# The opening stage of attention and two MLPs: all five engines in written order, weight preparation taken apart into single steps

## The chip, the cores and the metric

The kernel runs on one core of one Trainium2 chip. The metric is the device time of one execution in microseconds. Three runs of the kernel before took 616.21, 618.01 and 620.59 us; the median, 618.01 us, is the time that the change is measured against.

## What is computed

A decayed linear attention over 2 batches, 8 heads, 768 positions and 64 channels, then two MLPs on its 1536 tokens of 512 channels: one gated by a sigmoid (1536 wide), one with an ELU (2048 wide). All in float32.

```python
for b in range(nb):                       # blocks of the sequence
    intra = (qb @ kb.T * Dmask) @ vb
    inter = (qb * lam_pow) @ kv_state
    out[:, :, sl] = intra + inter
    kv_state = lam_block * kv_state + (kb * rev_pow).T @ vb
x = attention output as (tokens, 512)
x = (sigmoid(x @ w_gate) * (x @ w_val)) @ w_out
h = x @ w_in
y = where(h > 0, h, exp(min(h, 0)) - 1) @ w_out2
```

## The kernel before

The weights arrive as 64-bit floats; each load brings 1 MB (`load_w`, line 61) into the one buffer `w64`. `fetch` turns it into float32 in the one buffer `w32` with three instructions: ScalarE L71, VectorE L72 and L73. A later load of weights waits in SP's queue until L73 of the one before has read `w64`. Each float32 product is made of three matmuls of float32r halves, high and low, and the input products of the MLPs use a seven-product scheme (M1 to M7, line 181; one such product on 256 tokens is one step of six matmuls, and `ORDER` is the order in which the steps run). `prep_pair` therefore forms sums of weight blocks on GpSimd (t25 at L81, three parts of t3 at L83 to L85), rounds them to high halves on ScalarE (L91) and forms the low halves on VectorE or GpSimd (L92). The first two blocks of weights, of gate (wG) and value (wV), are needed as soon as two chunks of attention are done.

The opening stage handles the sequence in six chunks c of 128 positions. For each chunk and batch b (written here as two digits after the name: x10 is x of chunk 1, batch 0):

- TensorE: u (the chunk's part of the state, L300), st (scores, L287), x (output, L317, and from chunk 1 on L322 for the part from the state).
- ScalarE: kd (keys times decay, 8 instructions, L276), the copies of x to `xa` (L327, L329), the high halves of x (`x11h`, `x22h`, L142), of sums (`x143h`) and of xt (`xPh`, both L153).
- VectorE: pr (scores times mask, L293), sn (state, L307, L310), the low halves of x (L143), sums (L147), xt (L149).
- GpSimd: ql (queries times decay, L280, two buffers, released by x), and the low halves `x143l` and `xPl` (L154).

The stage has three groups of 14 steps of the MLP (gate, then value, each M2 M5 M1 M4 M3 M7 M6), on tokens of chunks 0 and 1, 2 and 3, 4 and 5. They become available after chunks 1, 3 and 5, and `fill(k)` puts the next k of them into TensorE's order between the attention's matmuls; what is left runs after chunk 5. While nothing of that kind is available (chunks 0 and 1), `warm_up(3)` puts three matmuls on zeros there, 24 in all, besides the 24 ahead of the loop.

In this stage only TensorE and SP (which issues every DMA) run in the order in which the program stands; a planner orders the other three engines by its own estimate of times, with high priority for attention. After chunk 5 (`start.close()`) it orders all engines.

SP's order before: lam, tin and nat of chunk 0 (tin in two halves), w_gate block 0, tin and nat of chunk 1, of chunk 2, w_val block 0, chunk 3, and so on. tin holds keys and queries, nat keys and values.

Of the kernel before, what the change touches and what calls it, by code (L numbers as in the profile page):

```python
# [30 lines left out]
def tile_decay_attention_two_mlps(  # L31
# [32 lines left out]
    def fetch(src, g, raw=None):  # L64

        raw = load_w(src, g) if raw is None else raw
        w = ws_p.tile([P, 1024], F32, tag="w32", name="w32")
        wi = w.bitcast(U32)  # L70
        nc.scalar.activation(w, raw[:, :, 1].bitcast(F32), AF.Prelu, scale=2.0 ** -112, alpha=2.0 ** 32)  # L71
        nc.vector.tensor_scalar(out=wi, in0=wi, scalar1=3, scalar2=None, op0=ALU.logical_shift_left)  # L72
        nc.vector.scalar_tensor_tensor(out=wi, in0=raw[:, :, 0], scalar=29, in1=wi,  # L73
                                       op0=ALU.logical_shift_right, op1=ALU.bitwise_or)
        return w

    def prep_pair(src, g, eng, eng_l=None, raw=None):
        eng_l = eng_l or eng
        raw = fetch(src, g, raw).rearrange("p (k a f) -> p k a f", k=KC, a=2)
# [6 lines left out]
        r = {}  # L86

        def split(tag, x, shape):
# [6 lines left out]
        h, l = split("25", t25, [P, 2, 2, P])  # L95
        r["M2"] = (h[:, :, 1], l[:, :, 1])
        r["M5"] = (h[:, :, 0], l[:, :, 0])
        h, l = split("3", t3, [P, 3, 2, P])
        r["M1"] = (h[:, 0], l[:, 0])
        r["M6"] = (h[:, 1], l[:, 1])  # L100
        r["M7"] = (h[:, 2], l[:, 2])
        r["M4"] = split("22", raw[:, 2:4, 1], [P, 2, P])
        r["M3"] = split("11", raw[:, 0:2, 0], [P, 2, P])
        return r

# [28 lines left out]
    def build_from_psum(ops, s, x0, x1, xa, t0, n, sums):  # L134


        sl = slice(t0, t0 + n)
        o = ops[s]
        a, b = slice(0, 2), slice(2, 4)
        with tc.high_priority(offset=HP):  # L140
            for key, src in (("11", x0[:, a]), ("22", x1[:, b])):
                nc.scalar.copy(o[key, "h"][:, :, sl], src)  # L142
                nc.vector.tensor_tensor(out=o[key, "l"][:, :, sl], in0=src, in1=o[key, "h"][:, :, sl].bitcast(F32),  # L143
                                        op=ALU.subtract)
            for k, (i0, i1, op) in enumerate(((x1[:, b], xa[:, a], ALU.add), (x0[:, b], xa[:, a], ALU.subtract),
                                              (x1[:, a], xa[:, 4:6], ALU.subtract))):
                nc.vector.tensor_tensor(out=sums[:, k], in0=i0, in1=i1, op=op)  # L147
            t = t_p.tile([P, 512], F32, tag="xt", name="xt", bufs=3).rearrange("p (k n) -> p k n", k=KC)
            nc.vector.tensor_tensor(out=t, in0=x1, in1=xa[:, 0:KC], op=ALU.add)  # L149
        for key, src, view in (("143", sums, (slice(None),) * 3), ("P", t, (slice(None),) * 2)):  # L150
            hi_, lo_ = (o[key, q][view + (sl,)] for q in "hl")
            with tc.high_priority(offset=HP):
                nc.scalar.copy(hi_, src)  # L153
                nc.gpsimd.tensor_tensor(out=lo_, in0=src, in1=hi_.bitcast(F32), op=ALU.subtract)  # L154
# [63 lines left out]
    with ExitStack() as actx:  # L218
# [4 lines left out]
        start.enter_context(tc.manual_schedule(engines={mybir.EngineType.PE, mybir.EngineType.SP}))  # L223
# [29 lines left out]

        one = low[:, 1536:1536 + CH]
# [17 lines left out]
        def front_pre(c):  # L272
# [4 lines left out]
            if c:  # L277
# [61 lines left out]

        idle = t_p.tile([P, 512], F32, tag="xt", name="idle", bufs=3).bitcast(BF16)[:, :512]  # L340
        nc.vector.memset(idle, 0.0)
# [8 lines left out]
        front_pre(0)  # L350
# [4 lines left out]
        wG = prep_pair(w_gate, 0, nc.gpsimd, nc.vector, w64)  # L355
        load(2)
        for c in range(NCH):
            if c == 0:
                wV = prep_pair(w_val, 0, nc.gpsimd, nc.gpsimd)
            more = c + 1 < NCH  # L360
            with tc.high_priority(offset=HP):
                if more:
                    state_mm(c)
                    state_post(c)
                    front_pre(c + 1)
                for b in range(2):
                    out_mm(c, b)
                    if c <= FIRST[0]:
                        warm_up(3)
                    if b == 0:  # L370
                        fill(2)
                    elif more:
                        fill(3)
                    if more:
                        front_mm(c + 1, b)
                        front_post(c + 1, b)
                    if c <= FIRST[0]:
                        warm_up(3)
                if c + 3 < NCH and c < 2:
                    load(c + 3)  # L380
                if c == 3:
                    load(c + 2)
            if c == 1:
                xops += new_xops(1)
# [3 lines left out]
            s, t0 = (0, c * CH) if c < 2 else (1, (c - 2) * CH)  # L388
            build_from_psum(xops, s, xps[c, 0], xps[c, 1], xas[c], t0, CH,
                            a2_p.tile([P, 3, 2, CH], F32, tag="sums", name="sums"))  # L390
# [124 lines left out]
    wG = prep_pair(w_gate, 1, nc.gpsimd)  # L515
# [146 lines left out]
```

## Time and profile before

| | |
|---|---|
| median of three runs | 618.01 us |
| the profiled execution | 620.34 us |
| its span, first to last instruction | 618.6 us |
| TensorE busy | 594.6 us, 96% |
| VectorE, ScalarE, GpSimd busy | 398.4, 298.7, 319.0 us |
| mean granted clock of TensorE | 0.986 of full |
| chunk 5's last x ends | 80.0 us into the span |

Busy times add the durations of instructions on one engine. Matmuls overlap in their records, so a TensorE that counts as busy may still wait. The granted clock is 1.00 at 2.4 GHz and 0.50 at 1.2 GHz; a mean between them is a stretch with both. The chain of work that ended last is followed back from the last instruction, at each step to what released it.

### The profile page before, as it was taken

The page shows a single profiled execution, that of the slowest core. Times are in us where ns is not written, and L with a number is a line of the kernel's source. Part 1 is how long each engine was busy: PE and PEld are TensorE (multiplying, and loading weights), DVE is VectorE, ACT ScalarE, POOL GpSimd, SP SyncE. Part 2 cuts the span into 40 slices and gives each one's busy share as a digit, 9 for nine tenths or more (in the row PEclk, how much of TensorE's full clock was granted, in tenths as well). Part 3 has the DMA queues.
Part 4 walks back from the last instruction along what each step waited for, and adds up shares of the span by engine and source line. Part 5 has one row for each costly group of instructions (what it writes and reads, how often), then busy time and mean ns, then how long its engine had stood idle before and what let it go on. Part 6 is the DMA issues. An engine that isn't in the chain of part 4 may idle for free.

```text
span 618.6 us, 9255 instructions
## 1 busy us (share of the span) xinstructions
PE 594.6 (96%) x3609; PEld 503.6 (81%) x3614; DVE 398.4 (64%) x681; ACT 298.7 (48%) x565; POOL 319.0 (52%) x262
## 2 busy tenths in 40 slices
PE   8899899999999999999997799979999999999997
PEld 4588799888888888888886688858888888888886
DVE  5979455455556465647746886565868676777574
ACT  3783246555415423515315868763728282816330
POOL 1788345968647538438335865663545445421100
PEclk9899899999999999999998999989999999999999
DMA  8935002323111111112300120421111211100005
GB/s 329 413 144 206 1 1 78 129 83 122 69 68 69 69 68 69 69 68 73 133 0 2 43 93 1 136 70 68 69 68 69 69 68 70 68 1 1 0 18 187
DMA packets 8828, 51.98 MB, mean 84 GB/s; under 512 B 1104, under 2 KB 1360, under 8 KB 3024
## 3 DMA queue, kind: packets, MB, share of 16 engines
q1 hardware_dynamic: 8784, 51.39, 22.4%
q8 instruction: 28, 0.46, 0.3%
q14 instruction: 16, 0.13, 0.1%
HBM read 48.24 MB, written 3.15 MB: 83 GB/s over the span
## 4 chain that ended last, share of the span: by engine, by line
PE 83%; DVE 9%; ACT 4%; issue 2%; DMA 1%; SPq 0%; DVEq 0%; ACTq 0%
PE xu L446 33%; PE A L181 19%; PE B L181 19%; PE C L181 6%; DVE w L72 2%; PE st L287 1%; DMA nat<-in_att 1%; PE x L322 1%; ACT kd L276 1%; PE x L317 1%; DVE w L73 1%; DVE acc L457 1%; ACT w L71 1%; DVE wt L190 1%; PE u L300 0%
## 5 line engine op out<-in xcount | busy, mean ns | idle before, releaser
L446 PE MATMUL xu<-gh,woh 128*128 128x512 f32 x310 | 120.8, 393 | 3.5 <-DVE acc L457 2.0
L457 DVE TENSOR_TENSOR acc<-xu,acc 128x512 f32<-128x512 f32 x120 | 81.9, 687 | 61.3 <-PE xu L446 60.6
L446 PE MATMUL xu<-gl,woh 128*128 128x512 f32 x310 | 120.8, 390 | 0.0
L446 PE MATMUL xu<-gh,wol 128*128 128x512 f32 x310 | 120.2, 388 | 0.0
L417 POOL TENSOR_TENSOR gl<-sig,gh 128x1024 fp32r<-128x1024 f32 (+1 forms) x38 | 79.2, 2100 | 41.5 <-ACT gh L416 41.5
L92 POOL TENSOR_TENSOR l<-t,h 128x512 fp32r<-128x512 f32 (+1 forms) x36 | 59.0, 1640 | 33.5 <-ACT h L91 28.5
L446 PEld LDWEIGHTS xu<-gh,woh 128*128 128x128 f32 x310 | 58.2, 189 | 16.7 <-DVE acc L457 4.4
L446 PEld LDWEIGHTS xu<-gh,wol 128*128 128x128 f32 x310 | 58.4, 188 | 12.2
L446 PEld LDWEIGHTS xu<-gl,woh 128*128 128x128 f32 x310 | 58.5, 189 | 10.4
L91 ACT CAST h<-t 128x512 fp32r<-128x512 f32 (+1 forms) x40 | 29.1, 730 | 54.3 <-POOL t L81 32.1
L92 POOL TENSOR_TENSOR l<-w,h 128x256 fp32r<-128x256 f32 x36 | 26.7, 748 | 55.5 <-ACT h L91 54.3
L73 DVE SCALAR_TENSOR_TENSOR w<-w,w 128x1024 uint32<-128x1024 uint32 x34 | 52.0, 1529 | 0.2
L416 ACT CAST gh<-sig 128x512 fp32r<-128x512 f32 (+1 forms) x58 | 43.8, 783 | 12.1 <-DVE sig L202 10.5
L190 DVE TENSOR_TENSOR wt<-B,wt 128x256 f32<-128x256 f32 (+1 forms) x44 | 22.6, 515 | 40.7 <-PE B L181 32.8
L72 DVE TENSOR_SCALAR w<-w 128x1024 uint32<-128x1024 uint32 x34 | 34.7, 1021 | 21.0 <-ACT w L71 20.9
L426 POOL TENSOR_TENSOR wol<-w,woh 128x512 fp32r<-128x512 f32 x26 | 33.1, 1297 | 29.2 <-ACT woh L424 29.1
L81 POOL TENSOR_TENSOR t<-w 128x512 f32<-128x512 f32 x20 | 26.0, 1302 | 38.5 <-DVE w L73 38.5
L71 ACT ACTIVATE w<-w 128x1024 f32<-128x1024 f32 x34 | 38.7, 1139 | 14.6 <-POOL l L92 7.2
L204 ACT ACTIVATE sig<-A 128x256 f32<-128x256 f32 (+1 forms) x34 | 16.0, 471 | 50.9 <-PE A L181 32.8
L91 ACT CAST h<-w 128x256 fp32r<-128x256 f32 x40 | 16.0, 407 | 47.2 <-PE A L181 22.7
L181 PE MATMUL A<-x11h,h 128*128 128x256 f32 (+1 forms) x88 | 29.8, 338 | 9.0 <-DVE sig L202 5.4
L205 ACT ACTIVATE sig<-sig 128x256 f32<-128x256 f32 (+1 forms) x68 | 34.2, 507 | 1.5
(169 smaller groups left out, 1566.0 us busy)
## 6 DMA issues: line engine op xcount, KB each, us to landing
w<-in_w_out SPq DMA_DIRECT2D x14, 1024.0 KB, 4.8
w<-in_w_in SPq DMA_DIRECT2D x8, 1024.0 KB, 4.7
nat<-in_att SPq DMA_DIRECT2D x6, 1024.0 KB, 9.6
w<-in_w_gate SPq DMA_DIRECT2D x6, 1024.0 KB, 4.8
w<-in_w_val SPq DMA_DIRECT2D x6, 1024.0 KB, 4.8
tin<-in_att SPq DMA_DIRECT2D x5, 1024.0 KB, 10.3
out_t<-o SPq DMA_DIRECT2D x11, 256.0 KB, 2.0
tin<-in_att SPq DMA_DIRECT2D x2, 512.0 KB, 4.8
```

What stands on the lines that cost most here:

```text
L71: nc.scalar.activation(w, raw[:, :, 1].bitcast(F32), AF.Prelu, scale=2.0 ** -112, alpha=2.0 ** 32)
L72: nc.vector.tensor_scalar(out=wi, in0=wi, scalar1=3, scalar2=None, op0=ALU.logical_shift_left)
L73: nc.vector.scalar_tensor_tensor(out=wi, in0=raw[:, :, 0], scalar=29, in1=wi, op0=ALU.logical_shift_right, op1=ALU.bitwise_or)
L91: nc.scalar.copy(hi, x)
L92: eng_l.tensor_tensor(out=lo, in0=x, in1=hi.bitcast(F32), op=ALU.subtract)
L181: nc.tensor.matmul(ps, lhsT=a[:, k], rhs=b_[:, k], start=first and k == 0 and j == 0, stop=k == 1 and j == 2, skip_group_check=True,)
L205: nc.scalar.add(dst, dst, -1.0)
L416: nc.scalar.copy(h, x)
L417: ((eng0 if s == 0 else eng) or eng or nc.gpsimd).tensor_tensor(out=l, in0=x, in1=h.bitcast(F32), op=ALU.subtract)
L426: (eng or nc.gpsimd).tensor_tensor(out=lo_[:, k], in0=raw[:, k], in1=hi_[:, k].bitcast(F32), op=ALU.subtract)
L446: nc.tensor.matmul(ps, lhsT=w[:, k, cs], rhs=g_cols(g, q, k, t_)[:, bs], start=k == 0 and j == 0, stop=k == 1 and j == 2)
L457: nc.vector.tensor_tensor(out=v, in0=p, in1=v, op=ALU.add)
```

## The change

In the opening stage every engine now runs in the order in which the program stands. `fetch` and `prep_pair` become generators (`fetch_steps`, `sum_steps`) whose steps the loop asks for one at a time, and `build_from_psum` is taken apart into the methods of `Operands`. The first step of wG (L71) stands after the keys of chunk 1, its L72 and L73 in chunk 1, its sums and halves at the end of chunk 1; wV is fetched in chunk 2 and split in chunk 3 (its load stands in chunk 1); block 1 of w_gate is fetched at the end of chunk 4, where the planner was free to take it earlier. Low halves of wG's and wV's t25 and single blocks are on VectorE, those of t3 on GpSimd. In SP's order chunk 1 now stands ahead of w_gate block 0. A small ScalarE instruction on a zeroed element stands at the very start, and the first load of the ScalarE table with it. The 24 `warm_up` matmuls inside the loop are gone, those ahead of it stay. `fill` puts in 3 steps in chunk 2 (5 before), 5 each in chunks 3 and 4, and 2 in chunk 5, so 15 of the 42 (17 before) stand inside the loop.

```diff
-        start.enter_context(tc.manual_schedule(engines={mybir.EngineType.PE, mybir.EngineType.SP}))
+        start.enter_context(tc.manual_schedule())
...
+        nc.vector.memset(low[:, 1664:1665], 0.0)
+        nc.scalar.mul(low[:, 1665:1666], low[:, 1664:1665], 1.0)
...
-        w64 = load_w(w_gate, 0)
         load(1)
+        w64G = load_w(w_gate, 0)
...
-        wG = prep_pair(w_gate, 0, nc.gpsimd, nc.vector, w64)
         load(2)
+        raw, wG, wV, raw1, parts = {}, {}, {}, {}, {}
+        fG = fetch_steps(w64G, raw)
         for c in range(NCH):
+            more = c + 1 < NCH
+            s, t0 = (0, c * CH) if c < 2 else (1, (c - 2) * CH)
+            if more:
+                state_mm(c)
+                if c != 2:
+                    queries(c + 1)
+            out_mm(c, 0)
+            o = parts[c] = Operands(xops, s, t0, CH, xas[c], a2_p.tile([P, 3, 2, CH], F32, tag="sums", name="sums"))
+            o.hi("11", xps[c, 0][:, 0:2])
+            if c == 1:
+                parts[0].split("143")
+            elif more:
+                state_post(c)
+            if c != 1:
+                o.first(xps[c, 0])
+            if more:
+                keys(c + 1)
             if c == 0:
-                wV = prep_pair(w_val, 0, nc.gpsimd, nc.gpsimd)
...
+                next(fG)
             if c == 1:
+                sG = sum_steps(raw["w"], wG, nc.gpsimd, nc.vector, nc.gpsimd, (0, 2, 1))
+            if c == 2:
+                parts[1].split("143")
+                queries(3)
+                parts[1].split("P")
+            if c > 2:
+                fill(2)
+            if more:
+                front_mm(c + 1, 0)
+                if c == 1:
+                    next(fG)
+                front_post(c + 1, 0)
+            if c == 1:
+                next(fG)
+                next(sG)
+                parts[0].split("P")
+                state_post(c)
+                o.first(xps[c, 0])
+                w64V = load_w(w_val, 0)
+            if c == 2:
+                fV = fetch_steps(w64V, raw)
+                next(fV)
+            out_mm(c, 1)
+            o.hi("22", xps[c, 1][:, 2:4])
+            if c == 3:
+                for _ in sV:
+                    pass
+            if c > 1 and more:
+                fill(3)
+            if more:
+                front_mm(c + 1, 1)
+                front_post(c + 1, 1)
+            o.second(xps[c, 1])
+            if c == 1:
+                for _ in sG:
+                    pass
                 xops += new_xops(1)
...
+            if c == 2:
+                for _ in fV:
+                    pass
+                sV = sum_steps(raw["w"], wV, nc.gpsimd, nc.vector, nc.gpsimd, (0, 2, 1))
+                next(sV)
+            if c > 1:
+                o.split("143")
+                o.split("P")
+            if c in (0, 1, 3):
+                load(3 if c == 0 else 4 if c == 1 else 5)
+            if c == 4:
+                wG1 = fetch(w_gate, 1)
...
-    wG = prep_pair(w_gate, 1, nc.gpsimd)
+    wG = prep_sums(wG1, nc.gpsimd)
```

The new steps that the loop calls (`hi` rounds one block of x on ScalarE, `lo` and the sums run on VectorE, `split` is ScalarE, then GpSimd):

```python
def first(self, x0):      # sums[:, 1], then lo("11")
def second(self, x1):     # sums[:, 0], sums[:, 2], xt, then lo("22")
def split(self, key):     # "143" or "P": high half, low half
```

## Rows read from the trace of the kernel before

**Rows 1.** The page's busy times, shares of the span and counts of each engine.

```profile
PE 594.6 (96%) x3609; PEld 503.6 (81%) x3614; DVE 398.4 (64%) x681; ACT 298.7 (48%) x565; POOL 319.0 (52%) x262
```

**Rows 2.** Windows: start:end, length, busy us (instructions) per engine, clock, DMA share, GB/s.

```profile
11.45:22.00 10.55, 8.23 (x91) 5.43 (x91) 7.61 (x11) 7.84 (x23) 7.45 (x6) 1.00 1.01 422
22.00:26.00 4.00, 3.64 (x42) 2.64 (x45) 3.58 (x8) 2.10 (x4) 0.41 (x2) 0.62 1.01 420
...
38.58:68.50 29.92, 29.01 (x389) 25.76 (x388) 23.05 (x44) 14.33 (x33) 23.69 (x20) 1.00 0.30 114
68.50:74.20 5.70, 3.86 (x27) 3.21 (x25) 2.42 (x7) 1.72 (x3) 3.20 (x3) 0.70 0.00 0
...
80.00:100.00 20.00, 19.73 (x160) 19.29 (x161) 9.97 (x22) 12.00 (x26) 11.23 (x9) 1.00 0.04 9
100.00:200.00 100.00, 100.00 (x527) 86.00 (x526) 52.88 (x87) 47.43 (x77) 69.86 (x57) 1.00 0.26 94
```

**Rows 3.** The same view of the warm-up matmuls alone (L346), from u00 on.

```profile
11.45:79.96 68.51, 6.20 (x21) 1.77 (x24) 0.95 0.50 198
```

**Rows 4.** The chain that ended last, pieces in time: start us, us, what.

```profile
2.16 7.28 DMA nat<-in_att
9.51 1.28 ACT L276
10.80 2.45 ACT kd L276 x8
...
14.36 0.71 DVE w L72
...
17.19 0.68 DVE sn L307
...
18.53 2.24 DVE l L92 x2
...
81.59 0.73 PE A L181 x6
```

**Rows 5.** Timeline of TensorE, landmarks: start us, us, engine line op out<-in.

```profile
26.37 1.04 PE L317 MATMUL x<-pr,nat 128*64 128x128 f32 x16
...
36.59 1.04 PE L317 MATMUL x<-pr,nat 128*64 128x128 f32 x16
...
46.77 1.15 PE L300 MATMUL u<-nat,kd 128*64 128x64 f32 x32
...
55.96 0.38 PE L181 MATMUL A<-x11h,h 128*128 128x256 f32 x1
...
72.17 2.08 PE L287 MATMUL st<-tin 64*128 64x128 f32 x16
...
78.87 1.09 PE L322 MATMUL x<-ql,sn 64*64 64x128 f32 x16
```

**Rows 6.** Timeline of VectorE and GpSimd around 44 us, [idle before].

```profile
43.51 1.32 POOL L280 TENSOR_TENSOR ql<-tin,low 128x512 f32<-128x512 f32 x1
...
43.67 4.73 DVE L72 TENSOR_SCALAR w<-w 128x1024 uint32<-128x1024 uint32 x1 [0.98 <-ACT w L71]
...
46.55 1.29 POOL L280 TENSOR_TENSOR ql<-tin,low 128x512 f32<-128x512 f32 x1
```

**Rows 7.** Groups, 11.45 to 80 us: shapes xcount | busy us, mean ns | idle before.

```profile
L153 ACT CAST x143h<-sums 128x768 fp32r<-128x768 f32 x5 | 4.2, 831 | 8.0 <-DVE sums L147 8.0
...
L327 ACT COPY xa<-x 128x512 f32<-128x512 f32 x6 | 3.5, 584 | 7.9 <-PE x L322 7.1 <-PE x L317 0.7
...
L142 ACT CAST x11h<-x 128x256 fp32r<-128x256 f32 x6 | 2.3, 377 | 0.0
...
L280 POOL TENSOR_TENSOR ql<-tin,low 128x512 f32<-128x512 f32 x10 | 14.2, 1428 | 19.9 <-DMA tin<-in_att 13.2 <-PE x L322 6.0 <-POOL xPl L154 0.7
L154 POOL TENSOR_TENSOR x143l<-sums,x143h 128x768 fp32r<-128x768 f32 x5 | 9.2, 1846 | 5.0 <-ACT x143h L153 4.9
...
L81 POOL TENSOR_TENSOR t<-w 128x512 f32<-128x512 f32 x3 | 3.9, 1284 | 2.0 <-DVE w L73 2.0
```

More of the change, by code (lines that the diff above doesn't have):

```diff
@@ L62, in load_w, with fetch_steps, fetch, sum_steps @@
         return raw
-    def fetch(src, g, raw=None):
-        raw = load_w(src, g) if raw is None else raw
-        w = ws_p.tile([P, 1024], F32, tag="w32", name="w32")
+    def fetch_steps(raw, out):
+        w = out["w"] = ws_p.tile([P, 1024], F32, tag="w32", name="w32")
         wi = w.bitcast(U32)
         nc.scalar.activation(w, raw[:, :, 1].bitcast(F32), AF.Prelu, scale=2.0 ** -112, alpha=2.0 ** 32)
+        yield
         nc.vector.tensor_scalar(out=wi, in0=wi, scalar1=3, scalar2=None, op0=ALU.logical_shift_left)
+        yield
         nc.vector.scalar_tensor_tensor(out=wi, in0=raw[:, :, 0], scalar=29, in1=wi,
                                        op0=ALU.logical_shift_right, op1=ALU.bitwise_or)
-        return w
-    def prep_pair(src, g, eng, eng_l=None, raw=None):
+        yield
+    def fetch(src, g, raw=None):
+        out = {}
+        for _ in fetch_steps(load_w(src, g) if raw is None else raw, out):
+            pass
+        return out["w"]
+    def sum_steps(raw, r, eng, eng_l=None, eng_3=None, order=(0, 1, 2)):
         eng_l = eng_l or eng
-        raw = fetch(src, g, raw).rearrange("p (k a f) -> p k a f", k=KC, a=2)
+        raw = raw.rearrange("p (k a f) -> p k a f", k=KC, a=2)
         t25 = ws_p.tile([P, 2, 2, P], F32, tag="t25", name="t25")
@@ L93, in split, with prep_sums, prep_pair @@
             return hi, lo
[L95 to L103, printed above, removed]
-        return r
+        for k in order:
+            if k == 0:
+                h, l = split("25", t25, [P, 2, 2, P])
+                r["M2"] = (h[:, :, 1], l[:, :, 1])
+                r["M5"] = (h[:, :, 0], l[:, :, 0])
+            elif k == 1:
+                h, l = split("3", t3, [P, 3, 2, P], eng_3 or eng_l)
+                r["M1"] = (h[:, 0], l[:, 0])
+                r["M6"] = (h[:, 1], l[:, 1])
+                r["M7"] = (h[:, 2], l[:, 2])
+            else:
+                r["M4"] = split("22", raw[:, 2:4, 1], [P, 2, P])
+                r["M3"] = split("11", raw[:, 0:2, 0], [P, 2, P])
+            yield
+    def prep_sums(raw, eng, eng_l=None):
+        r = {}
+        for _ in sum_steps(raw, r, eng, eng_l):
+            pass
+        return r
+    def prep_pair(src, g, eng, eng_l=None):
+        return prep_sums(fetch(src, g), eng, eng_l)
     def new_xops(*subs):
@@ L132, in x_operand @@
         return o[k, "h"], o[k, "l"]
[L134 to L154, printed above, removed]
@@ new lines, in tile_decay_attention_two_mlps, with __init__, hi, lo @@
+    class Operands:
+        def __init__(self, ops, s, t0, n, xa, sums):
+            self.o, self.sl, self.xa, self.sums = ops[s], slice(t0, t0 + n), xa, sums
+        def hi(self, key, src):
+            nc.scalar.copy(self.o[key, "h"][:, :, self.sl], src)
+        def lo(self, key, src):
+            nc.vector.tensor_tensor(out=self.o[key, "l"][:, :, self.sl], in0=src,
+                                    in1=self.o[key, "h"][:, :, self.sl].bitcast(F32), op=ALU.subtract)
+        def first(self, x0):
+            nc.vector.tensor_tensor(out=self.sums[:, 1], in0=x0[:, 2:4], in1=self.xa[:, 0:2], op=ALU.subtract)
+            self.lo("11", x0[:, 0:2])
+        def second(self, x1):
+            nc.vector.tensor_tensor(out=self.sums[:, 0], in0=x1[:, 2:4], in1=self.xa[:, 0:2], op=ALU.add)
+            nc.vector.tensor_tensor(out=self.sums[:, 2], in0=x1[:, 0:2], in1=self.xa[:, 4:6], op=ALU.subtract)
+            self.t = t_p.tile([P, 512], F32, tag="xt", name="xt", bufs=3).rearrange("p (k n) -> p k n", k=KC)
+            nc.vector.tensor_tensor(out=self.t, in0=x1, in1=self.xa[:, 0:KC], op=ALU.add)
+            self.lo("22", x1[:, 2:4])
+        def split(self, key):
+            src, view = (self.sums, (slice(None),) * 3) if key == "143" else (self.t, (slice(None),) * 2)
+            hi_, lo_ = (self.o[key, q][view + (self.sl,)] for q in "hl")
+            nc.scalar.copy(hi_, src)
+            nc.gpsimd.tensor_tensor(out=lo_, in0=src, in1=hi_.bitcast(F32), op=ALU.subtract)
@@ L252, in tile_decay_attention_two_mlps @@
         load(0, True)
+        idle = t_p.tile([P, 512], F32, tag="xt", name="idle", bufs=3).bitcast(BF16)[:, :512]
+        nc.vector.memset(idle, 0.0)
+        nc.vector.memset(low[:, 1664:1665], 0.0)
+        nc.scalar.mul(low[:, 1665:1666], low[:, 1664:1665], 1.0)
         one = low[:, 1536:1536 + CH]
@@ L337, in fill @@
                     fills.pop(0)()
-        idle = t_p.tile([P, 512], F32, tag="xt", name="idle", bufs=3).bitcast(BF16)[:, :512]
-        nc.vector.memset(idle, 0.0)
         warm = ps0.tile([P, 512], F32, tag="A0", name="warm")
@@ L354, in tile_decay_attention_two_mlps @@
             warm_up(5)
-        wG = prep_pair(w_gate, 0, nc.gpsimd, nc.vector, w64)
         load(2)
+        raw, wG, wV, raw1, parts = {}, {}, {}, {}, {}
+        fG = fetch_steps(w64G, raw)
         for c in range(NCH):
-            if c == 0:
-                wV = prep_pair(w_val, 0, nc.gpsimd, nc.gpsimd)
[L360 to L382, printed above, removed]
-            if c == 1:
+            more = c + 1 < NCH
[15 more added lines that the diff above has]
+                keys(c + 1)
+            if c == 0:
+                next(fG)
+            if c == 1:
+                sG = sum_steps(raw["w"], wG, nc.gpsimd, nc.vector, nc.gpsimd, (0, 2, 1))
[33 more added lines that the diff above has]
+                for _ in sG:
+                    pass
```

15 lines of the change are left out of this document (7 added, 8 removed).

## The prediction

> **What bounds the kernel now.** I read the busy times first: TensorE is busy for 96% of the span, no other engine for more than 64% [rows 1]. From 100 us on it is busy without a gap for a long time, and from 80 to 100 us it lacks 0.27 us [rows 2]. The change touches nothing there but the weights that are fetched ahead. So the question is how early TensorE gets through the attention, that is when chunk 5's last x ends: at 79.96 us [rows 5].
>
> Next I read the stretch from u00, at 11.45 us, to that point, 68.5 us. Its useful work at the full clock is 5 u of 1.15, 10 st of 1.04 (half of the 2.08 seen at half clock), 12 x of 1.04 and 10 of 1.09, and 17 steps of 0.73 [rows 4, 5]: 5.8 + 10.4 + 12.5 + 10.9 + 12.4 = 52.0 us. So 16.5 us are lost, and no change of order can gain more than that here. Where they go: 6.2 us are matmuls on zeros [rows 3]; TensorE idles 2.3 us up to 22 us, 0.4 in the next window, 0.9 from 38.6 to 68.5 and 1.8 around 70 [rows 2]; and it runs at 1.2 GHz in two places. A mean clock of 0.62 over 4.0 us is 3.0 us at half, 1.5 us of work lost; 0.70 over 5.7 us is 3.4 us at half, 1.7 lost [rows 2].
>
> Last I read what ends the waits at the start. The chain runs through nat of chunk 0 (landed at 9.44), the load of the ScalarE table (1.28), kd0 (2.45), then the preparation of wG: L72 from 14.36 on and VectorE's other work on it, which stands ahead of sn (17.19) and again, as 2.24 us of low halves, ahead of the next scores [rows 4].
>
> **The parts, and their costs.**
>
> *Table.* With the table loaded while ScalarE waits for nat anyway, kd0 ends at about 11.95 and not 13.25 [rows 4]. The warm-up matmuls ahead of u00 end at 11.45, so u00 ends at about 12.7 and x00 1.04 later, at 13.8: the whole 1.28 us. The cover is the 9.4 us wait for nat; nothing else is due on ScalarE.
>
> *Order of loads.* nat1 becomes the fourth megabyte of SP's queue. Before, tin1 was the fourth, and its arrival released ql after 13.2 us of idle time, at 14.5 [rows 7]. At the 420 to 422 GB/s of these windows [rows 2] a megabyte takes 2.5 us, so w_gate block 0 lands near 17, tin2 near 19.5, nat2 near 22 (estimates). L71 comes after kd1, near 17.2, so the later weights cost nothing; a late w_gate would hold the copies of x01 behind it, one for one.
>
> *Out of VectorE's way.* In the new order ScalarE takes xa (0.58), x11h (0.38) and kd1 (2.45) straight after x00 [rows 4, 7]: kd1 ends at 17.2. VectorE has sn done by 13.5. st11 ends near 17.6, u1 at 18.7, and x10 starts there: before at 26.37 [rows 5], a gain of 7.7. No matmuls on zeros stand between.
>
> *Chunk 1.* x10 to 20.8, st20 to 21.9 (tin2 is there), x11 to 24.0, st21 to 25.0. Meanwhile ScalarE takes xa, x11h, x143h (0.83) and kd2 (2.45) from 20.8 on, to 25.0. VectorE puts L72 and L73 between the scores and sn, which is done by 25.7. So u2 runs to 26.9 and x20 starts there, before at 36.59 [rows 5]: gain 9.7.
>
> *First new stall.* The steps of wG now stand behind attention on GpSimd. Its second ql of chunk 2 must wait for x11 (24.0). Behind it come x143l of chunk 0 (1.85), then t25 (1.28) and the three parts of t3, each a little over half of that (2.2 in all) [rows 7]: done near 30.9. ScalarE, in written order, rounds t3 only then, to 31.8, and behind it stand xa and x11h of chunk 2, kd3 and at last x143h of chunk 1: 31.8 + 0.58 + 0.38 + 2.45 + 0.83 = 36.0. x143l of chunk 1 takes GpSimd to 37.9. The third step of the first fill, M1, needs it. TensorE has done x20, st30, x21, M2 and M5 by about 33.6, so it idles about 4.2 us; without ScalarE's 3.1 us of waiting for t25 and t3 it would be 1.2. After M1 and st31, u3 starts at 39.6. Before it started at 46.77, with two more steps done (1.46): the gain is down to 5.7. Behind an idle stretch of 1.84 us the row of before shows the clock halved for 3.4 us, 1.7 lost [rows 2]; I take the same here: 4.0.
>
> *Second new stall.* In chunk 3, M4's sigmoid stands behind kd4 and the sigmoid's table (1.28, as in [rows 4]), and M7 waits for it. The next step, M2 of the value product, needs M7's sum off VectorE, which now stands behind three low halves of wV, and those behind t25 and the casts. By the same walk M2 starts near 54.0, 3.7 us after M6, before at 55.96 [rows 5]: gain 2.0. Its low end I put at 0.6: two dependent instructions like x11h's 0.38 [rows 7] and an estimated 0.6 for their hand-overs, less the 0.73 of M6 between them. Then the clock halves again, but before lost 1.8 idle and 1.7 of clock near 70, which the new fill, with other work between M7 and M2, mostly avoids. Chunk 5's last x ends near 74.6 with two steps fewer done, so 76.1: gain 3.9.
>
> *L72 behind GpSimd.* Once in this stage L72 took 4.73 us where wG's took 0.71 [rows 4]: it started at 43.67, while GpSimd worked without a break until 47.84 [rows 6]. The new order places L72 of wG near 20.6 and of wV near 43.4, where GpSimd waits for x10 or for L73 itself. I take 0.7 for both. If either is caught, it costs up to 4.0. The Trainium skill ("SBUF — State Buffer", section "Who interferes with whom") says that GpSimd and a VectorE instruction of this kind share a pair of ports and that the second blocks until the first finishes. By that rule L72 would have waited only for the first ql, to 44.83, some 1.2 us; the row shows it waiting through everything that GpSimd had queued, so the measurement is the worse of the two. By the page the cost of being caught would be 1.2.
>
> *Behind the stage.* Block 1 of w_gate, fetched late, is needed when 27 steps more are done, some 20 us later; its load, L71 to L73 and sums take about 12. The hand-over shifts with TensorE, at 0; the planner may lay the rest out otherwise, which I bound by 2 us either way, from the 0.27 idle in 80 to 100 us and the 1.84 of the worst gap.
>
> *Sum.* The walk gives 3.9. Its first stall lies between 1.2 and 4.2, its second between 0.6 and 3.7; I keep the first and put the second at its middle, 2.2: 3.9 + 1.5 = 5.4. The profiled execution took 620.34, 2.3 over the median; that difference lies in no stage that I can name, so I take 5.4 off the median: **612.6 us**. If both stalls are at their low ends and neither halves the clock, the gain is 3.9 + 3.0 + 3.1 + 3.4 = 13.4, within the 16.5 that there are: 604.6.
>
> **Rivals.**
>
> *The stalls hardly appear* (0.34). GpSimd and ScalarE run ahead of my walk, M1 and M2 follow at once: gains 6.5 to 13.4, time 605 to 611.5, about 608. For it: ScalarE and GpSimd are half idle before. Against: both have single-file queues now, with kd ahead of x143h.
>
> *The gain is lost behind* (0.15). The stage ends early, but an L72 is caught (4.0) and its stall halves the clock (1.7), or the next stage's weights are late by as much: 5.4 - 5.7, about 618.
>
> *Slower: the clock, without the zeros* (0.07). From u00 to the first steps there are some 20 groups of 1.04 to 1.15. At 1.2 GHz each costs about 1.0 more (st 2.08 [rows 5]). If all ran so it would be 20 - 5.4 more, about 632; it decides against the change from 6 groups, and by over 1% from 12. For it: the clock fell once with the zeros there, around 22 us [rows 2]. Against: the walk leaves no gap over 0.8 us before 33 us, and from 38.6 to 68.5 the same groups run without zeros at 1.00. The Trainium skill ("TensorE: Matmul & The Clock Gate", section "What's actually happening") says the clock follows how busy the array has lately been, halved when idle; the trace agrees, and by that rule the two stalls cost clock, not the start.
>
> **How the numbers follow.** My own case, 611 to 616, has 0.44; the three rivals 0.34, 0.15 and 0.07. The range takes in the low ends of both stalls and the lost gain: 605 to 619. A measurement can tell about 1%, 6.2 us, from no change: faster means below 611.8, slower above 624.2. Faster is the first rival and a little of my own case, 0.40; slower 0.07; the rest, 0.53, is within.
>
> **What would show it.** x10 starts near 18.7 and x20 near 27: right on the start. An idle TensorE ahead of M1 near 34 to 38 and of M2 near 50 to 54, each with a halved clock behind: right on the stalls. Chunk 5's last x near 73 to 75. Wrong if the clock is low between 12 and 30 us, if an L72 lasts over 2 us, or if TensorE is idle between 75 and 105 us.

## The result, and the profile after

The changed kernel takes 623.81 us, the median of nine runs (620.72 to 626.00). Nine runs of the kernel before gave 616.24. The ratio, estimated from all of these runs, is 1.0115 with a 95% interval of 1.0084 to 1.0146. Two later comparisons gave 1.0080 [1.0048, 1.0112] and 1.0090 [1.0064, 1.0116]. So the kernel became about 1% slower; 612.6 us was predicted, and the range (605 to 619) does not hold the time.

| | before | after |
|---|---|---|
| profiled execution | 620.34 us | 623.34 us |
| its span | 618.6 us | 621.6 us |
| mean granted clock | 0.986 | 0.978 |
| chunk 5's last x ends | 79.96 us, 17 steps done | 75.89 us, 15 steps done |
| first matmul of the output product (xu) starts | 101.79 us | 106.66 us |
| from there to the end of the span | 516.8 us | 514.9 us |

The last two lines place the loss. From xu on, after is even 1.9 us shorter; in the other traces of both kernels that part takes 514 to 515.1 us. So all of the loss arises before xu, and most of it behind chunk 5's last x. From that x to xu after takes 30.8 us and before 21.8. Two steps more are left to do in after, 1.46 us, so 30.8 - 21.8 - 1.46 = 7.5 us are lost there. The prediction put this at 0.

In the views of after the lines are those of the changed kernel: L70, L72 and L74 are the fetch, L89 to L93 the sums of weight blocks, L99 and L100 their high and low halves. L324 is st, L330 pr, L337 u, L354 and L359 x. L211 is a step, L218, L220 and L222 gather the products of M2, M5 and M1 in `wt`, L228 adds `wt` to M7 and M6, L230 is the sigmoid and L232 the product with it. L163 and L166 are the halves of x, L170 and L174 to L177 the sums of x, L183 and L184 their halves.

These are TensorE's landmarks in the timeline of after, as in [rows 5], with the idle time and what ended it in brackets:

```profile
18.81 1.05 PE L354 MATMUL x<-pr,nat 128*64 128x128 f32 x16
...
26.51 1.07 PE L354 MATMUL x<-pr,nat 128*64 128x128 f32 x16
...
35.84 0.58 PE L211 MATMUL C<-x143h,h 128*128 128x256 f32 x1 [2.47 <-ACT x143h L183]
...
37.76 0.58 PE L211 MATMUL C<-x143l,h 128*128 128x256 f32 x1 [1.34 <-POOL x143l L184]
...
55.38 0.39 PE L211 MATMUL A<-x11h,h 128*128 128x256 f32 x1 [3.93 <-ACT sig L230]
...
74.80 1.09 PE L359 MATMUL x<-ql,sn 64*64 64x128 f32 x16
...
80.94 0.55 PE L211 MATMUL B<-x22h,h 128*128 128x256 f32 x1 [2.70 <-DVE x22l L166]
...
91.32 0.39 PE L211 MATMUL B<-x143h,h 128*128 128x256 f32 x1 [0.67 <-DVE wt L220]
```

x10 starts at 18.81 (18.7 forecast) and x20 at 26.51 (26.9): the start went as worked out. Then come three idle places: M1 near 36, the value product's M2 at 55, and, behind the last x, M5 of the second group's gate product at 81. The first two were forecast; the third was not.

The windows of after, with columns as in [rows 2]:

```profile
11.45:22.00 10.55, 10.22 (x170) 8.61 (x170) 6.13 (x13) 6.54 (x19) 3.49 (x3) 1.00 1.01 421
...
26.00:38.58 12.58, 8.77 (x122) 7.47 (x118) 9.76 (x19) 8.53 (x22) 11.21 (x9) 0.88 0.65 255
38.58:50.00 11.42, 11.12 (x145) 9.67 (x145) 8.03 (x18) 6.52 (x16) 6.75 (x8) 0.84 0.31 99
50.00:60.00 10.00, 6.07 (x70) 5.42 (x71) 5.58 (x8) 3.46 (x9) 7.46 (x5) 0.83 0.49 205
...
80.00:90.00 10.00, 8.97 (x50) 8.72 (x51) 2.94 (x7) 3.89 (x8) 6.68 (x6) 0.67 0.19 81
90.00:100.00 10.00, 8.99 (x71) 8.44 (x70) 4.18 (x10) 3.12 (x7) 2.69 (x3) 1.00 0.00 1
```

The start is dense and at 1.00 without the zeros. Behind each idle place the clock is halved for a while. From the clock column, 12.58 x (1 - 0.88) / 0.5 = 3.0 us at half, 1.5 lost; the next windows give 1.8, 1.7 and, for 80 to 90 us, 6.6 at half and 3.3 lost. Behind the last x that makes 4.2 us idle (0.47, 2.70, 0.67 and 0.34) and 3.3 of clock, less the 0.3 that before idles there: 7.2 of the 7.5 us.

**The third idle place.** VectorE (DVE), ScalarE and GpSimd in after, around 75 us:

```profile
73.46 1.16 ACT L70 ACTIVATE w<-w 128x1024 f32<-128x1024 f32 x1
...
74.66 0.86 DVE L72 TENSOR_SCALAR w<-w 128x1024 uint32<-128x1024 uint32 x1 [1.56 <-ACT w L70]
75.55 2.19 DVE L74 SCALAR_TENSOR_TENSOR w<-w,w 128x1024 uint32<-128x1024 uint32 x1
...
79.12 0.41 DVE L174 TENSOR_TENSOR sums<-x,xa 128x256 f32<-128x256 f32 x1
...
80.38 0.41 DVE L166 TENSOR_TENSOR x22l<-x,x22h 128x256 fp32r<-128x256 f32 x1
...
74.92 1.74 POOL L184 TENSOR_TENSOR xPl<-xt,xPh 128x512 fp32r<-128x512 f32 x1
```

This is the fetch of block 1 of w_gate. It stands at the end of chunk 4 and so ahead of everything that VectorE does for chunk 5. The last x ends at 75.89 and its copy xa at 76.3, when the four instructions of `second` (three sums, then x22l) could begin. VectorE is on L74 until 77.74; L170, x11l, L228 and L232, which the program also wrote ahead of `second`, follow, and `second` starts at 79.12: 2.8 us late. TensorE waits 2.70 us for x22l. By the program's order this M5 works on chunks 2 and 3, and so not on chunk 5's x22l, but it starts 0.15 us behind it here, and again in the runs below where block 1 is fetched elsewhere with 15 steps. Why the program ties the two together is not shown. The weights themselves were not urgent: GpSimd has their sums ready at 81.1 us and forms the first low half of them only at 96.5, when TensorE has let go of the buffer.

The kernel before has the same fetch. Its planner placed it some 30 us earlier, around the L72 of [rows 6]. Its load was issued at 33.5 us; ScalarE and VectorE follow:

```profile
42.47 1.17 ACT L71 ACTIVATE w<-w 128x1024 f32<-128x1024 f32 x1
48.43 1.23 DVE L73 SCALAR_TENSOR_TENSOR w<-w,w 128x1024 uint32<-128x1024 uint32 x1
```

It holds VectorE from 43.67 to 49.66 us there, longer than in after. But from 38.6 to 68.5 us TensorE's only wait is one of 0.8 us, of st for pr.

### The profile page after: what moved, and what is told of

The parts are those of the page before. It is cut to its first block, busy times and chain, and to the rows that moved or that the text cites. A ratio compares the mean times of both kernels' runs of the same rounds, so it can differ in the third digit from the quotient of the medians.

```text
span 621.6 us, 9211 instructions
## 1 busy us (share of the span) xinstructions
PE 592.9 (95%) x3590; PEld 505.7 (81%) x3590; DVE 397.9 (64%) x684; ACT 298.4 (48%) x566; POOL 320.2 (52%) x260
## 4 chain that ended last, share of the span: by engine, by line
PE 85%; DVE 7%; ACT 4%; issue 2%; POOL 2%; DVEq 0%; POOLq 0%; ACTq 0%
PE xu L520 33%; PE B L211 19%; PE A L211 19%; PE C L211 7%; PE st L324 2%; PE warm L380 1%; PE u L337 1%; PE x L354 1%; PE x L359 1%; DVE w L72 1%; POOL x143l L184 1%; DVE wt L220 1%; DVE l L100 1%; DVE acc L531 1%; DVE sums L566 0%
## 5 line engine op out<-in xcount | busy, mean ns | idle before, releaser
L100 POOL TENSOR_TENSOR l<-t,h 128x768 fp32r<-128x768 f32 (+1 forms) x36 | 59.7, 1658 | 40.8 <-ACT h L99 28.1
L520 PEld LDWEIGHTS xu<-gl,woh 128*128 128x128 f32 x310 | 58.7, 189 | 11.2 <-DVE gl L491 0.8
L99 ACT CAST h<-t 128x512 fp32r<-128x512 f32 (+1 forms) x40 | 29.3, 731 | 58.3 <-POOL t L89 35.2
L100 POOL TENSOR_TENSOR l<-w,h 128x256 fp32r<-128x256 f32 x34 | 25.3, 751 | 53.6 <-ACT h L99 53.0
L74 DVE SCALAR_TENSOR_TENSOR w<-w,w 128x1024 uint32<-128x1024 uint32 x34 | 52.0, 1530 | 0.2
L220 DVE TENSOR_TENSOR wt<-B,wt 128x256 f32<-128x256 f32 (+1 forms) x44 | 22.6, 516 | 43.9 <-PE B L211 36.8
L70 ACT ACTIVATE w<-w 128x1024 f32<-128x1024 f32 x34 | 38.7, 1137 | 16.5 <-POOL l L100 7.7
L89 POOL TENSOR_TENSOR t<-w 128x512 f32<-128x512 f32 x20 | 26.3, 1316 | 39.2 <-DVE w L74 39.2
L72 DVE TENSOR_SCALAR w<-w 128x1024 uint32<-128x1024 uint32 x34 | 30.5, 897 | 20.7 <-ACT w L70 20.7
L99 ACT CAST h<-w 128x256 fp32r<-128x256 f32 x40 | 16.0, 408 | 45.8 <-PE A L211 22.5
L211 PE MATMUL A<-x11h,h 128*128 128x256 f32 (+1 forms) x88 | 29.4, 334 | 9.0 <-ACT sig L230 3.9
L211 PE MATMUL B<-x22h,h 128*128 128x256 f32 (+1 forms) x88 | 29.7, 338 | 6.4 <-DVE x22l L166 2.7
## 6 DMA issues: line engine op xcount, KB each, us to landing
nat<-in_att SPq DMA_DIRECT2D x6, 1024.0 KB, 11.2
```

Source lines behind the costliest of these rows:

```text
L211: nc.tensor.matmul(ps, lhsT=a[:, k], rhs=b_[:, k], start=first and k == 0 and j == 0, stop=k == 1 and j == 2, skip_group_check=True,)
L220: nc.vector.tensor_tensor(out=pair.wt[r], in0=ps, in1=pair.wt[r], op=ALU.add)
L520: nc.tensor.matmul(ps, lhsT=w[:, k, cs], rhs=g_cols(g, q, k, t_)[:, bs], start=k == 0 and j == 0, stop=k == 1 and j == 2)
```

## The experiments

Theory: three places where an engine in written order comes late (M1, M2, and M5 for x22l) each cost TensorE idle time and a halved clock, and nothing else in the change costs. The rivals are: the missing zeros cost clock; only one of the places counts; the two steps fewer inside chunk 5 are the cause. Medians are in us, ratios are to the kernel before in the same comparison, with 95% intervals.

**The two kernels again.** Neither was edited.

> The kernel before, unchanged, for a second trace. Its first trace took 620.34 us, while the median of nine runs is 616.24, so it may hold some 4 us that a usual run does not. If those lie behind the opening stage (after 102 us), this trace reaches the first xu near 102 us again and ends near 616. If they lie in the opening stage, the first xu comes near 98.

This is one run of before. It took 614.3 us, less than any of the 24 runs of before beside it (616.01 to 620.57, median 618.34). Its trace has the same work, but these rows differ:

```profile
22.00:26.00 4.00, 3.73 (x67) 3.00 (x67) 3.58 (x9) 1.96 (x4) 0.40 (x2) 1.00 1.02 424
...
68.50:74.20 5.70, 5.23 (x64) 4.63 (x65) 2.14 (x6) 1.44 (x4) 2.84 (x2) 1.00 0.00 0
...
75.65 1.09 PE L322 MATMUL x<-ql,sn 64*64 64x128 f32 x16
...
98.58 0.40 PE L446 MATMUL xu<-gh,woh 128*128 128x512 f32 x1
```

The two stretches of halved clock in [rows 2] are gone, the last x ends at 76.7 and xu starts 3.2 us earlier. So 3.2 of the 16.5 us that the prediction counted as lost are lost in some executions and not in others. This execution is below all the others and the first trace's (620.34) is above most, so a usual one lies between the two.

> The changed kernel, unchanged, beside the runs of this call. It should again be slower than before by 0.8 to 1.5%, with TensorE idle ahead of M1 (about 4 us, near 33 us), ahead of the value's M2 (about 4 us, near 51) and ahead of a step of the second group near 78 (2.7 us); the first xu comes near 105 to 107 us.

It took 623.26 us, a ratio of 1.0080. The last x ends at 78.0 and xu starts at 108.65, 30.7 us later. The loss behind the stage is that of the first trace.

> The changed kernel once more, unedited, on the same chip as the three runs that each mend a part of it: ratio 1.008 to 1.0115 as in its first two comparisons, first xu 30.7 us behind chunk 5's last x, waits for x143h and x143l, for M7's sigmoid and for x22l as before.

It took 624.30 us, a ratio of 1.0090. xu starts at 107.53, 30.8 us behind the last x, and the same three waits are there. It is the first corner of the square below.

**One place at a time.** M1 one fill later in chunk 3:

```diff
-                fill(2)                     # c > 2
+                fill(3 if c == 3 else 2)
-                fill(3)
+                fill(2 if c == 2 else 3)
```

> The changed kernel, but the step M1 of the gate product stands in chunk 3's first fill, not in chunk 2's. Theory: M1 waits for x143h behind kd3, and everything behind it in TensorE's order waits with it; moved, st31 starts near 35.8 us, when pr30 is done, not at 39.1. The stage gains about 2.5 us, and up to 1.7 more if the shorter idle stretch leaves the clock up: 620 to 621.5. Rival: the stage is bound by ScalarE or VectorE in chunk 3 anyway (kd4, the sigmoid's table), and the wait only moves to M4 or M7: under 1 us.

It took 622.10 us, a ratio of 1.0057 [1.0038, 1.0075]. The waits for x143h and x143l (2.5 and 1.3) are gone; instead st of chunk 3 waits 1.8 us for pr. The clock from 26 to 50 us is 0.93, where the changed kernel has 0.86. M2 and x22l wait as before.

M7 and its sum ahead of the other low halves of wV:

```diff
+            if c == 3:
+                next(sV)
             if c > 1 and more:
                 fill(3)
+            if c == 3:                      # these two lines stood ahead of fill(3)
+                for _ in sV:
+                    pass
```

> The changed kernel, but in chunk 3 only the first low half of wV stands ahead of the steps M7, M6 and M2; the other three stand behind. Theory: M2 waits 3.9 us at 51.2 us because M7's sum stands on VectorE behind three low halves (51.06 to 54.5, held up by GpSimd); now M2 starts near 52.6, not 55.4, and with the idle stretch near 1.2 us the clock stays up: gain 2.8 to 4.6 us, 619 to 621. Rival: M2 waits for ScalarE's queue instead; then under 1 us.

It took 620.12 us, a ratio of 1.0030 [1.0011, 1.0048]. The waits for the sigmoid fall from 4.7 (longest 3.9) to 2.4 (longest 1.5), the clock from 50 to 76 us rises from 0.93 to 1.00, and xu starts at 103.26. The sum that M2 waits for is L228; in the changed kernel ScalarE's table and the low halves stood ahead of it:

```profile
48.02 1.28 ACT L230 ACT_TABLE_LOAD   x1
...
51.06 0.69 DVE L100 TENSOR_TENSOR l<-t,h 128x512 fp32r<-128x512 f32 x1 [2.19 <-ACT h L99]
51.67 2.89 DVE L100 TENSOR_TENSOR l<-w,h 128x256 fp32r<-128x256 f32 x2
54.48 0.42 DVE L228 TENSOR_TENSOR A<-A,wt 128x256 f32<-128x256 f32 x1
```

Block 1 of w_gate fetched behind chunk 5, where the planner may place it:

```diff
-            if c == 4:
-                wG1 = fetch(w_gate, 1)
-    wG = prep_sums(wG1, nc.gpsimd)
+    wG = prep_pair(w_gate, 1, nc.gpsimd)
```

> The changed kernel, but block 1 of w_gate is fetched behind chunk 5, where the planner places it. Theory: the written fetch in chunk 4 puts L72 and L74 ahead of chunk 5's work on VectorE (3.0 us there, until 77.67), so x22l comes at 80.8, TensorE idles 2.7 us, and its clock is halved until 86.6 (2.8 us of work). Then this run gains 5 to 7 us on the changed kernel, 617 to 619. Rival: the loss between 76 and 107 us comes from the planner's order of the steps that are left, whatever is fetched: then less than 1.5 us change, 622 to 625.

It took 621.27 us, a ratio of 1.0046 [1.0027, 1.0064]. The wait for x22l falls from 2.7 to 0.2, and the clock from 76 to 102 us is 1.00 (0.87 in after). But the planner put the conversion far ahead, into the second stall:

```profile
56.40 1.14 ACT L70 ACTIVATE w<-w 128x1024 f32<-128x1024 f32 x1 [3.11 <-DVE l L100]
57.43 0.37 ACT L230 ACTIVATE sig<-A 128x256 f32<-128x256 f32 x1
```

ScalarE does L70 ahead of M7's sigmoid, M2 waits 5.5 us, and xu starts only 1.2 us earlier than in after. This run moved the fetch, but into another wait, so its time doesn't give the fetch's price. It does show the stretch from the last x to xu without it: 25.8 us, 5.0 less than after, with the same 31 steps in it.

**The square.** Three runs with 15 steps stand beside the unedited kernel on one chip: both stalls mended (the edits of the two runs above on M1 and M7), the fetch moved alone, and both. The fetch is moved by this edit:

```diff
+            if c == 5:                      # straight behind chunk 5's fill
+                wG1 = fetch(w_gate, 1)
-            if c == 4:
-                wG1 = fetch(w_gate, 1)
```

> Of the changed kernel only the two first stalls are taken away: M1 one fill later in chunk 3, and M7 with its sum ahead of the other low halves of wV; 15 steps stay, and block 1 of w_gate stays in chunk 4. Theory (the three places add up, each with its own idle time and halved clock): 3.5 to 5 us less than the changed kernel, a ratio to the kernel before of 1.000 to 1.003, the wait for x22l (2.7 us) unchanged, first xu near 103. Rival (only the last place counts, the two earlier ones are made good while TensorE waits for x22l): within 1.5 us of the changed kernel, ratio 1.006 or more.

It took 617.54 us, a ratio of 0.9989 [0.9971, 1.0007], 6.8 us less than the changed kernel beside it. xu starts at 100.81, and the wait for x22l stays. The view gives who waited for whom, the us in all, the number of times and the longest wait:

```profile
PE B L211 <- DVE x22l L166: 2.7, 1, 2.7
PE st L324 <- DVE pr L330: 2.0, 2, 1.8
PE A L211 <- ACT sig L230: 1.6, 2, 1.1
```

> Of the changed kernel only the place of block 1 of w_gate is moved, from chunk 4 into chunk 5 behind its fill, in written order; the two first stalls and the 15 steps stay. Theory (the places add up): 2.5 to 4 us less than the changed kernel, ratio 1.002 to 1.006, the wait for x22l gone, and the two stalls (M1 some 3.8 us, M2 some 3.9 us) unchanged. Rival (the stalls ahead hide it): within 1 us of the changed kernel, ratio 1.007 or more.

It took 622.13 us, a ratio of 1.0052 [1.0036, 1.0068], 2.2 us less. xu starts at 104.59, 27.7 us behind the last x; the wait for x22l falls to 1.5, not to 0, since L72 and L74 still stand ahead of `second`, and the clock from 76 to 102 us is 0.93. My theory's 2.5 to 4 was a little too much.

> All three places of the changed kernel mended, and nothing else: as the run with the two stalls gone, and block 1 of w_gate fetched in chunk 5 behind its fill, in written order, with 15 steps. Theory (they add up): 7 to 9 us less than the changed kernel, ratio 0.992 to 0.997, first xu near 99, no idle piece of TensorE over 2 us between 22 and 98 us. Rival (the two steps more inside chunk 5 are needed as well): ratio 1.000 or more, with a wait ahead of chunk 5's last x.

It took 616.08 us, a ratio of 0.9946 [0.9924, 0.9967], 8.2 us less, where the two alone add up to 6.8 + 2.2 = 9.0. xu starts at 98.84, 8.7 us earlier, of 6.7 + 2.9. So the places add up within what the medians can tell, and no one hides another. With all three mended and the same 15 steps the kernel is a little faster than before, so the fewer steps can't be what made it slower.

The place behind the last x is not wholly mended, though. xu starts 28.0 us behind it; as in before it would be 21.8 + 1.46 = 23.3, so 4.7 of the 7.5 us are still lost. The wait for x22l is 1.50 of them, and five waits of 0.57 us and less, for the sigmoid and `wt`, make 1.96 (0.27 in before). What causes these, and the rest, no run shows.

**More steps in chunk 5.** As before the change, 17 steps are written inside the stage:

```diff
-                fill(2)
+                fill(4 if c == 5 else 2)
```

> The changed kernel, but fill in chunk 5 puts in four steps, so that 17 stand inside the loop, as before. Theory: the steps M5 and M1 of the second group, left behind the loop, wait there for chunk 5's last work on VectorE, which L72 and L74 of w_gate hold up; inside the loop they run before it. The idle 2.7 us near 78 and the halved clock behind it go: first xu near 101 to 103 us, 4 to 5.5 us faster than the changed kernel. Rival: the wait belongs to whatever step is the first behind the loop, and only moves: under 1.5 us.

It took 624.33 us, a ratio of 1.0104. There is no gain. The trace shows 19 steps ahead of the last x, and not 17: M4 and M7 of the second group, which stand behind the loop and are the planner's to place, run there too, ahead of M5 and M1. The same holds for the next four runs; in before and after the traces show 17 and 15, as written. So no run here shows what 17 steps would do. The wait for x22l is down to 0.2, but this M4 waits 1.8 us for `wt`, ScalarE's copy of M2's product, which stands behind L70, xa and x11h; the clock falls ahead of the last x, and that ends at 85.1. The wait has moved.

> The run with 17 steps, and beside it one instruction group moved: the fetch of block 1 of w_gate stands in chunk 5 behind its four steps, not at the end of chunk 4. Theory: it is this fetch (L70 on ScalarE, L72 and L74 on VectorE) in the written order that made the steps of chunk 5 wait, wherever they stood. Chunk 5's last x ends near 78 us (85.1 with the fetch at its old place), the clock is not halved between 76 and 85, the first xu comes near 100 to 101: 5 to 7 us faster than with 17 steps alone, about as fast as before. Rival: VectorE is full there anyway, with the sums of chunks 4 and 5; then the first xu stays at 105 to 107.

It took 625.47 us, a ratio of 1.0109. The clock from 76 to 102 us is now 1.00 and xu starts 1.35 us earlier than in the run above, but the time is no less. The two first stalls are there (2.5 + 1.3, and 5.0). Behind xu this trace takes 519.1 us instead of 514.2. The difference lies between 300 us and the end, where the planner orders all engines: TensorE idles 17.8 us there instead of 15.3, and its clock from 400 to 500 us is 0.97 instead of 1.00. Why is not known.

> Four edits at once: M1 in chunk 3, the low halves of wV but one behind M7, M6 and M2, 17 steps inside the loop, and the fetch of block 1 of w_gate at the end of chunk 5. Theory (each wait costs what the trace shows and they add): the last x of chunk 5 ends near 71 us, the first xu comes near 96 to 98, 8 to 10 us before the changed kernel's; time 613 to 616 on a chip where before takes 618, 0.4 to 0.8% under it. Rival: another queue takes over after the first two (kd4 and the sigmoid's table on ScalarE): first xu near 101, the same time as before.

It took 617.73 us, a ratio of 0.9991 [0.9973, 1.0008]. The clock is 1.00 from 11 to 76 us. L72 and L74 now hold up `wt` (L220) and so M3 of the second group's value product by 1.7 us, with the clock at 0.93 from 76 to 102.

> The run with four edits, but the fetch of block 1 stands behind chunk 5's four steps and ahead of its last x, where VectorE idled 1.8 us and ScalarE 3.4. Theory: the 1.7 us wait near 82 us and the halved clock behind it go: first xu near 96 to 97 (100.2), 3 to 4 us faster, 613.5 to 615 where before takes 618.4. Rival: the planner's order behind the loop waits for something else at once: under 1 us.

It took 613.90 us, a ratio of 0.9923 [0.9906, 0.9940], with the fetch straight behind chunk 5's written four steps. This version beats both kernels. VectorE's timeline there, and the windows from 50 to 102 us:

```profile
73.88 0.68 DVE L72 TENSOR_SCALAR w<-w 128x1024 uint32<-128x1024 uint32 x1
74.47 0.42 DVE L228 TENSOR_TENSOR A<-A,wt 128x256 f32<-128x256 f32 x1
74.81 1.22 DVE L74 SCALAR_TENSOR_TENSOR w<-w,w 128x1024 uint32<-128x1024 uint32 x1
76.27 0.42 DVE L174 TENSOR_TENSOR sums<-x,xa 128x256 f32<-128x256 f32 x1 [0.25 <-ACT x22h L163]
...
50.00:76.00 26.00, 23.12 (x284) 20.17 (x285) 19.29 (x40) 9.82 (x22) 14.16 (x10) 1.00 0.14 59
76.00:102.00 26.00, 23.80 (x182) 22.52 (x182) 13.10 (x31) 12.96 (x26) 16.90 (x14) 1.00 0.23 82
```

L72 and L74 are done by 76.03, while TensorE works on steps and the last x; `second` waits for its own input alone. The clock stays at 1.00, xu starts at 98.40.

> The run with four edits and the fetch moved, and the first small ScalarE instruction is a sigmoid, so that the table of the sigmoid is loaded at the start and not behind kd4. The load of 1.28 us ahead of M4's sigmoid goes: the wait of M7 near 47 us (1.15) goes with it: 0.8 to 1.3 us faster than the same with the first table, if nothing else holds M7. If M7 waits for its place on another queue, no difference.

It took 613.87 us, a ratio of 0.9922. The table load ahead of M7 is gone, yet the waits for the sigmoid are 3.2 us (1.8 in the run above), and there is no difference in time. M7's sum starts at 49.83 us, against 49.93 in the run above: ahead of it on VectorE stands the one low half left there, which took 2.27 us here (from 47.64) and 0.86 there (from 49.14). So the 1.28 was not what M2 waited for.

**Parts of the change in the kernel before.**

The matmuls on zeros are left out:

```diff
-                    if c <= FIRST[0]:
-                        warm_up(3)          # in both places of the loop
```

> The kernel before, without the 24 matmuls on zeros inside its loop, and nothing else changed. If they hold the clock up, the granted clock falls between 12 and 39 us and the kernel is 1 to 3 us slower. If they only fill idle time, as the path there runs over VectorE and ScalarE, the time stays within 0.2%. If they stand in the way, it is up to 1 us faster.

It took 615.36 us, a ratio of 0.9954 [0.9939, 0.9969]. Without the zeros the kernel before is faster, though its trace shows st waiting 4.3 us for pr and a clock of 0.50 from 22 to 26 us.

With the zeros left out, the table and the order of loads are changed as well:

```diff
+        nc.vector.memset(low[:, 1664:1665], 0.0)
+        nc.scalar.mul(low[:, 1665:1666], low[:, 1664:1665], 1.0)
-        w64 = load_w(w_gate, 0)
         load(1)
+        w64 = load_w(w_gate, 0)
```

> The kernel before with three parts of the change and the planner kept: no zeros in the loop, the table loaded at the start, chunk 1 ahead of w_gate block 0. If written order is what costs, this is the version to keep: 1 to 3 us under the same without table and loads (615.4). Against: w_gate lands 4.5 us later, and L71 to L73 then reach VectorE while chunk 1 needs it; then 1 to 3 us slower than that.

It took 617.99 us, a ratio of 0.9997 [0.9976, 1.0017], under the planner. Compared with the run above, table and order of loads don't help here: st waits 4.4 us for pr, M1 3.4 for x143l and M5 1.3 for x22l.

## Why the prediction was wrong, step by step

**Right: the start.** The table is loaded during the wait for nat, x00 ends at 13.81 (13.8 forecast), x10 and x20 come within 0.4 us of the walk. The windows show the zeros' place filled with attention at full clock, so the rival that the clock falls without them did not come about. In before their removal gained 0.5%, although there the clock did fall, to 0.50 from 22 to 26 us.

**Right: L72.** In after the three L72 of the stage take 0.69, 0.68 and 0.86 us; none is caught as in [rows 6].

**Right in mechanism: the first stall.** It was forecast from 33.6 to 37.9, 4.2 us. M1's product C waits 2.47 and 1.34, 3.81 in all, until 37.76. ScalarE did as walked: h of t3 behind GpSimd, xa, x11h, then kd3, then x143h:

```profile
31.14 0.83 ACT L99 CAST h<-t 128x768 fp32r<-128x768 f32 x1 [1.28 <-POOL t L93]
...
32.61 2.45 ACT L312 ACTIVATE kd<-nat,low 128x128 f32<-128x128 f32 x8
34.97 0.82 ACT L183 CAST x143h<-sums 128x768 fp32r<-128x768 f32 x1
```

The clock behind it cost 1.5 + 1.8 us by the windows, twice the 1.7 assumed.

**Mis-sized: the second stall.** The walk gave 3.7 us and M2 at 54.0; I took the middle of it and an argued low end, 2.2. It is 3.93, with M2 at 55.38. The walk was the better value; M2's 1.4 us beyond it were there almost whole when M6 ended, at 51.45 instead of 50.3. The low end of 0.6 took 0.6 us for hand-overs as an estimate, which [rows 7] doesn't give; where M7's sum was brought forward, M2 waited 1.1 to 1.5 us (2.7 in the run without the table load ahead of M7).

**Mis-sized: the gain in the stage.** Chunk 5's last x ends at 75.89 (74.6 by the walk, 73.1 by the sum), or 77.35 with two steps added: 2.6 us before 79.96 instead of 5.4. The same sum can be made from the other side: 64.4 us from 11.45 to that point, less 52.0 - 1.46 of useful work, leaves 13.9 lost, where before lost 16.5. Of these, 8.2 are idle at the marked places (0.45 ahead of u2, 3.81, 3.93) and 5.0 are clock. And the 16.5 is not the same in every execution: by before's second trace 13.3 are lost (76.7 - 11.45 - 52.0), and after's traces end the stage, with their two steps, at 77.4, 79.4 and 78.2. Against that trace the stage gained nothing.

**Wrong: "Behind the stage", at 0 with 2 us either way.** That is the step that failed, with 7.5 us (7.4 and 7.5 in the two other traces of after). It asked when block 1 is needed, found 20 us for a work of 12, and stopped. It did not ask what stands behind the fetch on its engine, nor where the planner had put it: its caught L72 of [rows 6] is this very fetch, at a time when TensorE had other work. In written order L72 and L74 hold up sums and x22l of chunk 5, whatever time the weights have. How much of the 7.5 the fetch explains is known only within bounds. From the last x to xu, moving it took back 3.0 us alone, 1.8 with both stalls mended, and 5.0 where the planner placed it; in time it was 2.2 and 1.5 us for the first two. Some 2.5 us stay even then, and their cause is open. The rival "lost behind" (0.15, about 618) had the place, but another mechanism (weights late or an L72 caught) and less than the price. The sentence on what would prove the prediction wrong, an idle TensorE between 75 and 105 us, names the place where it happened.

**The sum.** In the profiled executions: 2.6 gained in the stage, 7.5 lost behind it, 1.9 gained from xu on, in all 3.0 lost, which is 623.34 - 620.34. From the forecast of 612.6 to the median of 623.8 it is 11.2: 7.5 behind the stage, 2.8 that the stage gained less, 2.3 because a gain read from an execution of 620.34 was taken off a median of 618.01, and 0.5 between after's profiled execution and its median, less the 1.9. The experiments share out the loss another way: mending the two forecast stalls is worth 6.8 us, moving the fetch 2.2 alone and 1.5 on top of them. The forecast stalls are thus the larger part of what the change could have gained. They were counted, but against one execution of before that had lost up to 3 us more than others, and with the clock behind the first at half its cost.

**Left open.** What causes the part of the loss behind the last x that stays when the fetch is moved. Why moving the fetch in the version with more steps, without the other edits, gains nothing in time, though xu starts earlier. And which of table and order of loads takes back, in before, what the missing zeros give.

## What to carry to other kernels

When engines change from a planner to written order, every piece of work that is not urgent must be given a place by looking at what stands behind it on that engine, not at when its own result is needed; the place for it is a moment when that engine waits anyway. A long idle place of TensorE was paid twice here, by itself and by the clock behind it, so a walk's own value for a stall should stand in the sum, not a kinder middle. And a second trace of the kernel before shows which of its losses come back in every execution.

## What the runs showed of the hardware

The same idle time does not always cost clock. In both traces of the kernel before TensorE idles 1.84 us ahead of M2 near 70 us; in the first the clock behind it is halved [rows 2], in the second it stays at 1.00. The runs with both stalls mended are the same program up to 50 us; both leave TensorE idle 1.8 us ahead of st of chunk 3, and one is halved behind it and the other not, as the timelines and the windows 26 to 50 us of first the one with the fetch in chunk 4 and then the one with the fetch moved show:

```profile
36.16 2.67 PE L324 MATMUL st<-tin 64*128 64x128 f32 x16 [1.83 <-DVE pr L330]
26.00:50.00 24.00, 21.64 (x276) 19.07 (x277) 18.68 (x39) 16.41 (x41) 20.73 (x18) 0.86 0.52 185
```

```profile
36.09 1.75 PE L324 MATMUL st<-tin 64*128 64x128 f32 x16 [1.80 <-DVE pr L330]
26.00:50.00 24.00, 19.66 (x282) 17.08 (x282) 19.57 (x41) 16.66 (x41) 20.71 (x18) 1.00 0.61 231
```

So part of the spread of a kernel's times is whether its short gaps happen to cost clock: between the two traces of before this is 3.2 of the 6.0 us by which their spans differ (618.6 and 612.6). At the three long idle places of after, of 2.47 to 4.66 us, the clock was halved in all three of its traces.

L74 took 2.19 us at 75.55 while GpSimd's xPl ran beside it, and xPl 1.74; alone they take 1.22 and 1.28 in the same trace (at 44.75 and 63.30). The Trainium skill ("SBUF — State Buffer", section "Who interferes with whom") says that a VectorE instruction with two inputs in SBUF contends with a GpSimd instruction that reads SBUF; the trace agrees, and both pay.
